# Two-level Strassen gates in the fourth token group of a fused attention and feed-forward kernel

## The chip, the cores and the metric

The kernel runs on one core of one Trainium2 chip. The metric is the device time of one execution in microseconds (us); the time before is the median of three runs. One more execution was taken with the hardware profiler, and all views below are of that one.

## The reference, cut to what matters

Linear attention with a norm, then a feed-forward part whose two gates are multiplied without a nonlinearity. Everything is float32.

```python
# q, k, v: (8, 8, 576, 64); w1, w2: (512, 1024); w3: (1024, 1024); w_out: (1024, 512)
kv  = einsum('bhsd,bhse->bhde', k, v)
out = einsum('bhsd,bhde->bhse', q, kv)
x   = out / sqrt(mean(out * out, -1) + 1e-6) * g_norm
x   = x.transpose(0, 2, 1, 3).reshape(8 * 576, 512)
y   = ((x @ w1) * (x @ w2)) @ w3 @ w_out
```

## The kernel before

**Groups.** Each of the 8 batches gives 512 tokens to a group of its own; the 64 left over of each batch make a ninth group. The groups run in the order T = 0 to 6, then 8 (the left-over tokens), then 7. w3 and w_out are multiplied together once at the beginning (L678). After that each group does two things on TensorE: the *gates* (x times w1 and w2, multiplied with each other on VectorE) and the *projection* (the product times the folded w3 and w_out).

**Gates, one level.** A group has four parts p0 to p3 of the gate columns. `gates` runs each part as one level of a Strassen-Winograd scheme, `winograd`: seven products of 4 matmuls with 256 columns (L699), where seven blocks of the weights (a11, a12, a22 and the sums s1 to s4) meet seven of x (b11, b21, b22, t1 to t4). Between the products ScalarE copies results out of PSUM (`keep`, L712: p1, p5, u2, u3, each into one tile of its name), and VectorE adds and multiplies (L839, L840). The third product, s2 times t2, accumulates in the PSUM bank of the first, so TensorE may only begin it once p1 is kept; in the same way s4 waits for p5, s3 for u2, and a22 for u3. `between` is called twice in each part, after u2 and after c11, and runs the attention work of the next batch, one entry of `steps` at a time.

**Gates, two levels.** For the groups in IN_TWO, now T = 4, 5, 6, 8 and 7, the parts p0 and p1 are done together by `gates_of_two`: each of the seven products is itself split into seven, 49 products of one matmul with 128 columns (L953) for each of the two gates. It is run between parts p2 and p3. It needs sums of sums: those of x are made at the group's beginning (`sum_x`, L918 to L921); those of the weights are made once (`prepare_w`, a triple of vector operations L875, L876, L877 for each of seven products), stored into a scratch tensor w_l2 in DRAM (`store_w`, L868), and loaded back in five pieces for every such group (`load_w`, L899). `replace_a21` (L887) then overwrites the a21 blocks, which only one-level gates still need, with a further sum and stores three of them. Where the triples lie is written out by hand: one each behind the sums of p0, p1 and p2 of T = 2, two each behind p0 and p1 of T = 3; `replace_a21` is called in p2 of T = 3. A triple uses one of three buffers in turn, so that it can only be written when the store of the triple three before has landed. Each of its blocks goes out in a store of its own, 128 KB.

**Projection.** `project_twice` is a two-level scheme for every group but the first: seven times 14 matmuls with 128 columns (L1162). ScalarE copies (L1173, L1174); VectorE makes the sums of its inputs (L1120 to L1124) and finishes the outputs (L1258, L1201, L1202, and four steps L1183 to L1186 for each block of the output). finish(p5), finish(p1) and finish(u4) come last, at the beginning of the next group's gates; the next group's first keep writes the same tile as p1.

**Turns.** q and the attention's x are needed transposed. `turn_by_dma` copies the halves of each float32 apart (L297, L299), has the DMA engines transpose them (L301, on SyncE's queue), and copies them together again (L311). For the batches up to 4 the copies are GpSimd's, except those of batch 1's first half; for later ones they are ScalarE's, hung by `turns_by_scalar` behind named keeps: a key such as (0, 3) is the keep after product 3 of gate 0 in `gates_of_two`, ("p3", "u2") the keep u2 of part 3, ("proj", "u3") a keep of the projection. Batch T + 1 is turned in group T.

**Order.** TensorE, GpSimd and SyncE run in the order of the program. VectorE and ScalarE run in the order that a scheduler gives them, except in part p3 and the projection, where VectorE's order is as written; the scheduler can still put other operations between. `tc.issue_after(x)` holds what is issued in it behind x. Every engine's queue, SyncE's with its DMAs too, is worked off in order.

The lines that place the triples and the first call of `between` in this change:

```python
                with tc.issue_after(ops[-1].ins):
                    for _ in range({(2, 0): 1, (2, 1): 1, (2, 2): 1, (3, 0): 2, (3, 1): 2}.get((T, p), 0)):
                        next(preparing_w)
...
            if T == FIRST_OF_TWO - 1 and p == 2 and not replaced:
                replaced.append(True)
                replace_a21()
```

Of the kernel before, what the change touches and what calls it, by code (L numbers as in the profile page):

```python
# [22 lines left out]
def kernel(  # L23
# [32 lines left out]
    nc = tc.nc  # L56
    PSUM = bass.MemoryType.PSUM
    P = 128
# [3 lines left out]
    DF = w1.shape[1]  # L62
    NP = H // 2
    KF = DF // P
    FIRST_OF_TWO = 4
    NH = KF // 2
    J = 4
    G = J * P
# [19 lines left out]
    loaded, copies, adds = {}, {}, {}  # L88
# [437 lines left out]
    def turns_by_scalar(b):  # L526

        a, turning = batch(b), {}

        def at(key, *call):  # L530
            slots.setdefault(key, []).append(call)

        def begin(name, f, *args):
            turning[name] = f(*args, nc.scalar.copy)
            next(turning[name])
            if name[0] == "q":
                next(turning[name])
            elif name[2]:
                for r in range(2):
                    next(turning["x", name[1], r])  # L540

        def end(name):
            all_of(turning[name])
            if name[0] == "q" and name[1] != "left":
                batch(name[1]).load_ahead("q", name[2])

        for r in (2, 3):
            at((0, 0), begin, ("q", b, r), a.q_by_dma, r)
        if b % 2:
            at(("p2", "c21"), begin, ("q", "left"), a.q_left_by_dma)  # L550
            at((0, 3), end, ("q", "left"))
        at((0, 6), end, ("q", b, 2))
        at((1, 0), end, ("q", b, 3))
        for h, begins, ends in (
            (0, ((0, 3), (0, 3)), ((1, 3), (1, 3))),
            (1, (("p3", "p1"), ("p3", "p5")), (("p3", "c21"), ("proj", "p1"))),
        ):
            for r in range(2):
                at(begins[r], begin, ("x", h, r), a.x_part_by_dma, h, r)
                at(ends[r], end, ("x", h, r))  # L560
        if b + 1 < B:
            n = batch(b + 1)
            for r in range(2):
                at(("p3", "u2"), begin, ("q", b + 1, r), n.q_by_dma, r)
                at(("proj", ("u2", "u3")[r]), end, ("q", b + 1, r))

    def steps(b):

        a = batch(b)
        a.start()
        more = b + 1 < B
        fs, ends = ([[] for _ in range(8)] for _ in range(2))

        def turn(i, f, *args, next_group=False):

            t = []

            def begin():
                t.append(f(*args))
                next(t[0])
                next(t[0])

            fs[i].append((begin,))
            (to_end if next_group else ends[i + 1]).append((lambda: all_of(t[0]),))

        if to_end:

            ends[0] += [(lambda: nc.gpsimd.tensor_copy(tick, late["p5"][:, 0, 0:1]),), *to_end]
        to_end.clear()
        odd = b % 2
        by_scalar = b > FIRST_OF_TWO
        if b == 1:
            early.extend(a.q_two_by_dma(r) for r in (0, 1))
            q_first = list(early)
            fs[0].append((a.begin_kv, 0, 1))

            def end_first():  # L600
                for t in q_first:
                    with tc.issue_after(copies["kv"].ins):
                        next(t)
                    all_of(t)

            ends[1].append((end_first,))
        fs[1] += [(a.begin_kv, 2, 3), (a.finish, 0)]
        if b == 1:
            last = {}

            def begin(name, behind, f, *args):
                last[name] = f(*args)
                with tc.issue_after(copies[behind][-1].ins):
                    next(last[name])
                next(last[name])

            def end(name, behind):
                with tc.issue_after(copies[behind][-1].ins):
                    next(last[name], None)
                all_of(last[name])  # L620

            fs[2] += [(begin, f"q{r}", "u2", a.q_two_by_dma, r) for r in (2, 3)]
            fs[3] += [
                (begin, "x", "u3", a.x_by_dma, 0, nc.scalar.copy),
                (begin, "left", "u3", a.q_left_by_dma),
            ]
            ends[4] += [(end, "q2", "p1"), (end, "q3", "p5"), (end, "x", "u2")]
            ends[5].append((end, "left", "u3"))
        elif by_scalar:
            turns_by_scalar(b)  # L630
        else:
            turn(1, a.q_two_by_dma, 2, 3)
            turn(2, a.x_by_dma, 0)
            if odd:
                turn(1, a.q_left_by_dma)
        second = 5 if b == 1 else 4
        if more:
            fs[second].append((batch(b + 1).begin_kv, 0, 1))
        fs[second].append((a.finish, 1))
        if odd:  # L640
            fs[3 if by_scalar else second].append((a.product_left,))
        if b == 1:
            turn(6, a.x_by_dma, 1)
            turn(7, a.x_left_by_dma, next_group=True)
        else:
            if not by_scalar:
                turn(5, a.x_by_dma, 1)
            if odd:
                turn(5, a.x_left_by_dma, next_group=more)
        if more and not by_scalar:  # L650
            turn(7 if b == 1 else 5, batch(b + 1).q_two_by_dma, 0, 1, next_group=True)
        if more:
            fs[7 if odd else 0].append((load_q_left, b + 1))
        return iter([lambda s=e + f: [f(*args) for f, *args in s] for e, f in zip(ends, fs)])
# [107 lines left out]
    xb, wa, aa, ob = {}, {}, {}, {}  # L762
    xc = const.tile([P, 3, NP // 2, N], FP32, name="xc")
    free = {("w", 0): const.tile([P, 3, 2, NP // 2, P], FP32, name="ws0")}
    o_sbs, ab_sums, w3o_sums, streams, inner_sums = [], [], [], [], []
    PART = 7 * 2 * P

    def allocate():
# [5 lines left out]
    def allocate_projection():  # L774
# [17 lines left out]
            [w[:, 2 * PART:2 * PART + 256], w[:, 2 * PART + 256:2 * PART + 512], room[2][:, PART:PART + 256]],  # L792
        ]
        inner_sums.extend([t.rearrange("p (c t) -> p c t", c=2) for t in s] for s in spare)

    def parts(t):
        return [t[:, i] for i in range(3)]
# [67 lines left out]
    def store_w(n, key, src):  # L865
        dst = w_l2[:, 0:len(BLOCKS) * P].rearrange("p (w m) -> p w m", w=2)
        at = BLOCKS[0, n, key] * P
        nc.sync.dma_start(out=dst[:, :, at:at + P], in_=src)  # L868

    def prepare_w():  # L870

        for n, (name, _) in enumerate(PRODUCTS):
            a11, a12, a21, a22 = w_blocks(name)
            s1, s2, s4 = inner_sums[n % 3]
            nc.vector.tensor_add(s1, a21, a22)  # L875
            nc.vector.tensor_sub(s2, s1, a11)  # L876
            nc.vector.tensor_sub(s4, a12, s2)  # L877
            blocks = {"s1": s1, "s2": s2, "s4": s4, "a11": a11, "a12": a12, "a22": a22}
            for key, t in blocks.items():
                if (0, n, key) in BLOCKS:  # L880
                    store_w(n, key, t)
            yield

    def replace_a21():
        for n, (name, _) in enumerate(PRODUCTS):
            a11, _, a21, _ = w_blocks(name)
            nc.vector.tensor_sub(a21, a11, a21)  # L887
            if (0, n, "s3") in BLOCKS:
                store_w(n, "s3", a21)
# [493 lines left out]
    for n, T in enumerate(groups):  # L1383
        pieces = steps(T + 1) if n + 2 < NG else iter([])

        def between():
            if len(converted) < len(begun):
                with tc.issue_after(copies["u2"][-1].ins):
                    end_next()
            next(pieces, lambda: None)()  # L1390
            if T == 1:
                for _ in range(2):
                    if next(preparing, 0) == 0 and len(loaded_b) < 3:
                        load_b()
            if T == FIRST_OF_TWO - 1 and p == 2 and not replaced:
                replaced.append(True)
                replace_a21()

        if T in IN_TWO:
            p = 2  # L1400
# [9 lines left out]
            of_two = sum_ab_two()  # L1410
            for _ in range(2):
                of_two.pop(0)()
        for p in range(NF):
            if T in IN_TWO and p + 1 < NF:
                continue
            stage[0] = f"p{p}" if T in IN_TWO else None
            if T and p + 1 == NF:
                sum_1, sum_2, sum_4, sum_3 = sum_ab(p)
                following = {
# [50 lines left out]
            else:  # L1470
                ops = [step() for step in sum_ab(p)]
                with tc.issue_after(ops[-1].ins):
                    for _ in range({(2, 0): 1, (2, 1): 1, (2, 2): 1, (3, 0): 2, (3, 1): 2}.get((T, p), 0)):
                        next(preparing_w)
        last = n + 1 == NG
        if T:
            project_twice(
# [4 lines left out]
            continue  # L1482
        project(T, between)
        run(combine_x(1))
        preparing, preparing_w, replaced = prepare_b(), prepare_w(), []
        third = late_pool.tile([P, 3, 2, P], FP32, name="inner_sums")
        inner_sums.append([third[:, i] for i in range(3)])


# [28 lines left out]
```

## Time and profile before

| what | value |
|---|---|
| median of 3 runs | 753.99 us (753.05 to 754.78) |
| the profiled execution | 753.1 us, its span 751.3 us |
| TensorE busy | 743.1 us, 99% of the span |
| VectorE busy | 636.4 us, 85% |
| ScalarE busy | 322.2 us, 43% |
| GpSimd busy | 84.6 us, 11% |
| DMA | 160.94 MB, mean 214 GB/s |
| stores into w_l2 | 33 of 128 KB, 1.8 to 4.2 us to landing |
| DMA transposes L301 | 66, 2.7 to 6.5 us to landing |

How to read it: PE is the matmuls and PEld the weight loads of TensorE, which overlap them; DVE is VectorE, ACT ScalarE, POOL GpSimd, SP SyncE. A line number such as L699 is that of the kernel before. The chain that ended last is followed back from the last instruction to whatever released each one; a share of the span in it is time that can only be won there. An instruction's row has start, duration, engine, line, and in brackets how long its engine had been idle and who released it. Idle time of an engine that isn't on the chain costs nothing.

### The profile page before, as it was taken

Reading aid. Unit: us, or ns where it says so; the run is one execution under the profiler, and the core shown is the slowest. Engines: PE = TensorE matmul, PEld = TensorE weight load, DVE = VectorE, ACT = ScalarE, POOL = GpSimd, SP = SyncE. Lnnn points to the kernel's source line nnn. Section 1 sums busy time; section 2 is a strip of 40 time slices with the busy share of each in tenths; the row PEclk is TensorE's granted clock in tenths of the full one; section 3 lists DMA queues with packets and bytes.
Section 4 is the critical chain, followed back from the end, with each engine's and each line's share of the span. In section 5 each row is a group of like instructions: output and inputs, shape, how many; then the busy total and the mean of one; then the engine's idle time right before and its main releaser. Section 6 shows DMA issues by size and latency. Waiting matters only on the chain.

```text
span 751.3 us, 15612 instructions
## 1 busy us (share of the span) xinstructions
PE 743.1 (99%) x6155; PEld 659.0 (88%) x6155; DVE 636.4 (85%) x1301; ACT 322.2 (43%) x558; POOL 84.6 (11%) x83
## 2 busy tenths in 40 slices
PE   7999999999999999999999999999999999999998
PEld 5455788888899889988999999999999999999997
DVE  6977999648889679877798899889979997899897
ACT  6687878313222332233225753565367323222321
POOL 0000000222520442044201000100001000000000
PEclk9999999999999999999999999999999999999999
DMA  9996955349997947697468986799658663465354
GB/s 306 327 349 193 280 147 118 88 73 280 330 300 264 242 138 207 231 245 217 134 240 228 246 274 225 221 256 259 239 148 208 213 221 108 150 221 177 126 199 140
DMA packets 155245, 160.94 MB, mean 214 GB/s; under 512 B 87076, under 2 KB 140068, under 8 KB 155172
## 3 DMA queue, kind: packets, MB, share of 16 engines
q1 hardware_dynamic: 152720, 145.52, 65.8%
q10 hardware_dynamic: 2452, 14.42, 5.6%
q8 instruction: 49, 0.80, 0.4%
q14 instruction: 24, 0.20, 0.1%
HBM read 121.90 MB, written 20.71 MB: 190 GB/s over the span
## 4 chain that ended last, share of the span: by engine, by line
PE 96%; DMA 2%; DVE 2%; ACT 1%; issue 0%; SPq 0%; ACTq 0%
PE mm L699 45%; PE mm L1162 23%; PE mm L953 15%; PE mm L678 7%; PE at L340 3%; PE at L416 2%; DMA raw<-in_moe_w_out_dram 1%; PE at L665 1%; DMA raw<-in_moe_w_dram 0%; PE at L1213 0%; PE at L435 0%; PE at L359 0%; DVE c L839 0%; DVE chunks L174 0%; DVE inv L385 0%; DVE raw L875 0%
## 5 line engine op out<-in xcount | busy, mean ns | idle before, releaser
L699 PE MATMUL mm<-xT,w_sb 128*128 128x256 f32 x576 | 132.2, 379 | 0.0
L699 PEld LDWEIGHTS mm<-xT,w_sb 128*128 128x128 f32 x576 | 108.7, 190 | 14.8 <-issue 0.5
L699 PE MATMUL mm<-xc,ws 128*128 128x256 f32 x416 | 94.8, 380 | 0.4 <-ACT p L712 0.4
L699 PEld LDWEIGHTS mm<-xc,ws 128*128 128x128 f32 x416 | 78.8, 190 | 12.1 <-ACT p L712 1.5
L678 PE MATMUL mm<-chunks,ab 128*128 128x512 f32 x128 | 60.2, 603 | 1.4 <-DVE chunks L174 1.0
L712 ACT COPY u<-mm 128x512 f32<-128x512 f32 x46 | 27.0, 587 | 74.3 <-PE mm L699 58.9
L712 ACT COPY p<-mm 128x512 f32<-128x512 f32 x54 | 31.5, 586 | 53.2 <-PE mm L699 40.5
L699 PE MATMUL mm<-xc,w_sb 128*128 128x256 f32 x208 | 50.0, 383 | 0.0
L1162 PE MATMUL mm<-w3o_sb,ab 128*128 128x128 f32 x368 | 48.6, 275 | 0.0
L1173 ACT COPY u<-mm 128x512 f32<-128x512 f32 x23 | 13.5, 586 | 81.6 <-DVE raw L1186 47.7
L1162 PE MATMUL mm<-w3o_sb,raw 128*128 128x128 f32 x372 | 48.1, 275 | 0.0
L699 PE MATMUL mm<-xT,ws 128*128 128x256 f32 x192 | 45.8, 381 | 0.0
L1162 PEld LDWEIGHTS mm<-w3o_sb,ab 128*128 128x128 f32 x368 | 45.4, 192 | 0.4
L1162 PEld LDWEIGHTS mm<-w3o_sb,raw 128*128 128x128 f32 x372 | 44.8, 192 | 0.0
L699 PEld LDWEIGHTS mm<-xc,w_sb 128*128 128x128 f32 x208 | 38.9, 190 | 5.5
L678 PEld LDWEIGHTS mm<-chunks,ab 128*128 128x128 f32 x128 | 21.8, 190 | 23.9 <-issue 15.3
L840 DVE TENSOR_TENSOR ab<-c 128x256 f32<-128x256 f32 x78 | 40.7, 522 | 2.1
L385 DVE TENSOR_REDUCE inv<-sq 128x8 f32<-128x512 f32 (+1 forms) x40 | 24.1, 627 | 20.9 <-ACT sq L384 20.6
L834 ACT COPY c<-mm 128x256 f32<-128x256 f32 x26 | 9.7, 372 | 72.6 <-PE mm L699 72.6
L699 PEld LDWEIGHTS mm<-xT,ws 128*128 128x128 f32 x192 | 36.1, 190 | 5.0
L953 PE MATMUL mm<-ws,w3o_sb 128*128 128x128 f32 x250 | 38.5, 275 | 0.0
L297 POOL COPY xT<-xn 128x1024 uint16<-128x1024 uint16 x14 | 17.1, 1249 | 151.5 <-DVE xn L394 151.5
(249 smaller groups left out, 1627.6 us busy)
## 6 DMA issues: line engine op xcount, KB each, us to landing
w3o_sb<-w3o_l SPq DMA_DIRECT2D x18, 896.0 KB, 5.3
raw<-in_moe_w_dram SPq DMA_DIRECT2D x31, 512.0 KB, 7.1
raw<-w3o_l SPq DMA_DIRECT2D x15, 896.0 KB, 4.8
w3o_sb<-w_l SPq DMA_DIRECT2D x15, 896.0 KB, 5.3
w3o_sb<-w3o_l ACTq DMA_DIRECT2D x14, 896.0 KB, 4.6
k_sb<-in_k_dram SPq DMA_DIRECT2D x32, 256.0 KB, 4.5
v_sb<-in_v_dram SPq DMA_DIRECT2D x32, 256.0 KB, 4.8
q_sb<-in_q_dram SPq DMA_DIRECT2D x32, 256.0 KB, 3.6
```

What stands on the lines that cost most here:

```text
L297: copy(to, src.rearrange("p a n w -> p w a n"))
L340: nc.tensor.matmul(kv_ps[e * D:(e + 1) * D, r - rs[0], :], lhsT=k_sb[:, e, cols] if j < J else kl[:, 2 * r + e, :], rhs=v_sb[:, e, cols] i ...
L385: nc.vector.tensor_reduce(out=inv[:, i], in_=sq.rearrange("p (h d) -> p h d", d=D), axis=AX.X, op=ALU.add)
L416: nc.tensor.matmul(o_ps[l][tokens, n * D:(n + 1) * D], lhsT=qT[r][rows, e, i, tokens], rhs=kv_b[rows, e, r, :], start=True, stop=True,)
L678: nc.tensor.matmul(sums_ps[half][m], lhsT=w3T[half, c][:, m, :], rhs=chunks[:, c, 1, :], start=(c == 0), stop=(c == KF - 1),)
L699: nc.tensor.matmul(ps[:, u, :], lhsT=lhsT(a_name, u, c), rhs=rhs(b_name, c),  start=(u == 0 and c == 0 and to is None), stop=(c == chunks ...
L712: copies.setdefault(name, []).append(nc.scalar.copy(t, ps))
L834: copied = nc.scalar.copy(c, one[:, 0, :])
L840: nc.vector.tensor_mul(dst, c[:, 0, :], c[:, 1, :])
L953: nc.tensor.matmul(ps[place // 4][:, place % 4, :], lhsT=x, rhs=y, start=new and place // 4 not in seen, stop=True, skip_group_check=True,)
L1162: nc.tensor.matmul(to[:, i, :], lhsT=x[:, c, :], rhs=y[:, c, :], start=new and place // 4 not in seen, stop=(c == 1), skip_group_check=True,)
L1173: nc.scalar.copy(t[:, 0:4], ps[0])
```

## The change

T = 3 joins the groups with two-level gates (FIRST_OF_TWO is 3). All seven triples are made in T = 2: two at its beginning, two called from the first `between` of p1, three behind the sums of p1; `replace_a21` is called in the second `between` of p2 of T = 2. The sums of a triple now lie in a row in their buffer and go out in one store (in two for the buffer whose third piece lies elsewhere), and a11 with a12 in one: 18 stores instead of 33. For batch 3, turned in the one-level group T = 2, ScalarE gets a list of places of its own for the turns of q and x; batch 4 is turned in T = 3 in the way of the later ones.

```diff
-    FIRST_OF_TWO = 4
+    FIRST_OF_TWO = 3
...
+        if b > FIRST_OF_TWO:
+            q_begins, q_ends = ((0, 0), (0, 0)), ((0, 6), (1, 0))
+            left_q = ("p2", "c21"), (0, 3)
+            x_begins, x_ends = ((0, 3), (0, 3)), ((1, 3), (1, 3))
+        else:
+            q_begins, q_ends = (("p1", "p1"), ("p1", "p5")), (("p1", "u3"), ("p1", "u3"))
+            left_q = ("p0", "c21"), ("p2", "p5")
+            x_begins, x_ends = (("p1", "u2"), ("p1", "u2")), (("p1", "c21"), ("p2", "p1"))
...
-        by_scalar = b > FIRST_OF_TWO
+        by_scalar, in_two = b >= FIRST_OF_TWO, b > FIRST_OF_TWO
...
-        nc.sync.dma_start(out=dst[:, :, at:at + P], in_=src)
+        nc.sync.dma_start(out=dst[:, :, at:at + src.shape[2]], in_=src)
...
-            s1, s2, s4 = inner_sums[n % 3]
+            t = {key: t.rearrange("p (w n) -> p w n", w=2) for key, t in in_a_row[n % 3].items()}
+            s1, s2, s4 = t["s1"][:, :, 0:P], t["s1"][:, :, P:2 * P], t.get("s4", t["s1"])[:, :, -P:]
...
-            blocks = {"s1": s1, "s2": s2, "s4": s4, "a11": a11, "a12": a12, "a22": a22}
-            for key, t in blocks.items():
-                if (0, n, key) in BLOCKS:
-                    store_w(n, key, t)
+            for key in t:
+                store_w(n, key, t[key])
+            if (0, n, "a11") in BLOCKS:
+                store_w(n, "a11", wa[0][name].rearrange("p w c m -> p w (c m)"))
+                store_w(n, "a22", a22)
...
+        def prepare_some(pieces):
+            if T == FIRST_OF_TWO - 1:
+                for _ in range(pieces):
+                    next(preparing_w)
+                prepared.append(pieces)
...
+            if T == FIRST_OF_TWO - 1 and p == 1 and len(prepared) == 1:
+                prepare_some(2)
...
-            if T == FIRST_OF_TWO - 1 and p == 2 and not replaced:
+            if T == FIRST_OF_TWO - 1 and p == 2:
                 replaced.append(True)
-                replace_a21()
+                if len(replaced) == 2:
+                    replace_a21()
...
+        if T == FIRST_OF_TWO - 1:
+            with tc.issue_after(adds["out"].ins):
+                prepare_some(2)
...
-            stage[0] = f"p{p}" if T in IN_TWO else None
+            stage[0] = f"p{p}" if T in IN_TWO or T == FIRST_OF_TWO - 1 else None
...
-                    for _ in range({(2, 0): 1, (2, 1): 1, (2, 2): 1, (3, 0): 2, (3, 1): 2}.get((T, p), 0)):
-                        next(preparing_w)
+                    if p == 1:
+                        prepare_some(3)
```

More of the change, by code (lines that the diff above doesn't have):

```diff
@@ L545, in end @@
                 batch(name[1]).load_ahead("q", name[2])
+        if b > FIRST_OF_TWO:
[6 more added lines that the diff above has]
+            x_begins, x_ends = (("p1", "u2"), ("p1", "u2")), (("p1", "c21"), ("p2", "p1"))
         for r in (2, 3):
-            at((0, 0), begin, ("q", b, r), a.q_by_dma, r)
+            at(q_begins[r - 2], begin, ("q", b, r), a.q_by_dma, r)
         if b % 2:
[L550 to L553, printed above, removed]
+            at(left_q[0], begin, ("q", "left"), a.q_left_by_dma)
+            at(left_q[1], end, ("q", "left"))
+        for r in (2, 3):
+            at(q_ends[r - 2], end, ("q", b, r))
         for h, begins, ends in (
-            (0, ((0, 3), (0, 3)), ((1, 3), (1, 3))),
+            (0, x_begins, x_ends),
             (1, (("p3", "p1"), ("p3", "p5")), (("p3", "c21"), ("proj", "p1"))),
@@ L640, in steps @@
         if odd:
-            fs[3 if by_scalar else second].append((a.product_left,))
+            fs[3 if in_two else second].append((a.product_left,))
         if b == 1:
@@ L764 @@
     free = {("w", 0): const.tile([P, 3, 2, NP // 2, P], FP32, name="ws0")}
-    o_sbs, ab_sums, w3o_sums, streams, inner_sums = [], [], [], [], []
+    o_sbs, ab_sums, w3o_sums, streams, inner_sums, in_a_row = [], [], [], [], [], []
     PART = 7 * 2 * P
@@ L794, in allocate_projection @@
         inner_sums.extend([t.rearrange("p (c t) -> p c t", c=2) for t in s] for s in spare)
+        in_a_row.append({"s1": room[1][:, 1024:PART]})
+        in_a_row.append({"s1": w[:, 2 * PART:2 * PART + 512], "s4": spare[1][2]})
     def parts(t):
@@ L1484 @@
         run(combine_x(1))
-        preparing, preparing_w, replaced = prepare_b(), prepare_w(), []
+        preparing, preparing_w, prepared, replaced = prepare_b(), prepare_w(), [], []
         third = late_pool.tile([P, 3, 2, P], FP32, name="inner_sums")
         inner_sums.append([third[:, i] for i in range(3)])
+        in_a_row.append({"s1": third.rearrange("p s c t -> p (s c t)")})
 _INS = ['q', 'k', 'v', 'g_norm', 'moe_w1', 'moe_w2', 'moe_w3', 'moe_w_out']
```

## The prediction

> **What bounds the kernel now.** I read the page's rows of busy time and its chain first, then the chain in order of time to find where each group begins and ends, then the busy time of each engine by group, and last the instructions in order of time around the places that the change touches. Groups are named by T; the fourth is T = 3, the third T = 2.
>
> ```profile
> PE 743.1 (99%) x6155; PEld 659.0 (88%) x6155; DVE 636.4 (85%) x1301; ACT 322.2 (43%) x558; POOL 84.6 (11%) x83
> PE 96%; DMA 2%; DVE 2%; ACT 1%; issue 0%; SPq 0%; ACTq 0%
> ```
>
> TensorE is the bound: 96% of the chain that ended last is its own work. So a gain has to be TensorE work removed, and a cost is a place where TensorE has to wait. The next view gives busy time by group, T = 1 to T = 6 (T = 3 is the third row, T = 5 the fifth):
>
> ```profile
> 163.00:239.30 76.30, 76.30 (x633) 69.61 (x632) 62.09 (x126) 20.39 (x43) 20.46 (x19) 1.00 0.99 292
> 239.27:315.78 76.51, 76.38 (x662) 69.33 (x661) 60.35 (x126) 21.24 (x46) 22.48 (x20) 1.00 0.72 200
> 315.78:391.85 76.07, 75.71 (x629) 68.74 (x629) 60.67 (x127) 20.18 (x43) 22.42 (x19) 1.00 0.73 209
> 391.85:465.90 74.05, 74.05 (x745) 70.30 (x745) 67.73 (x149) 41.26 (x70) 4.42 (x4) 1.00 0.82 234
> 465.90:539.05 73.15, 73.15 (x713) 69.58 (x713) 65.09 (x146) 38.87 (x65) 2.43 (x3) 1.00 0.81 240
> 539.05:611.71 72.66, 72.66 (x705) 68.97 (x705) 66.32 (x151) 36.45 (x62) 2.32 (x3) 1.00 0.70 211
> ```
>
> After stretch and length come PE, PEld, DVE, ACT and POOL busy. The granted clock is 1.00 in all. TensorE fills every group; the fourth has only 0.36 us of idle. T = 5 is what the fourth group is turned into: also a group before an even batch, with the same attention work on TensorE (no left-over rows), two-level gates, turns on ScalarE. It is 2.92 us shorter. The chain in order of time shows where:
>
> ```profile
> 239.27 10.60 PE mm L699 x48
> ...
> 350.77 19.19 PE mm L699 x88
> 369.96 21.88 PE mm L1162 x196
> 391.85 10.36 PE mm L699 x48
> ...
> 480.59 15.63 PE mm L953 x140
> ```
>
> Counts are matmuls and weight loads together, so 88 is 44 matmuls of 256 columns at 436 ns, and 140 is 70 matmuls of 128 columns at 223 ns.
>
> **The change, part by part.**
>
> *Gates of the fourth group.* Gone are 2 parts x 7 products x 4 = 56 matmuls of 256 columns (L699): 56 x 0.436 = 24.4 us. New are 2 x 49 = 98 of 128 columns (L953): 98 x 0.223 = 21.9 us. That is -2.5 us. The Trainium skill speaks against this step: "TensorE: Matmul & The Clock Gate", section "Back-to-back issue gap", gives a stream of load-and-multiply pairs about 81 ns at 128 columns and 131 ns at 512, so half the columns cost far more than half the time. Interpolated, 256 columns would be 98 ns, a ratio of 0.83, and the estimate from that page is 98 x 0.436 x 0.83 = 35.5 us: 11 us slower. In this trace's stream the ratio is 223/436 = 0.51, in five groups of the same code. I take the trace. The direct difference of whole groups, T = 5 against T = 3, is 73.15 - 76.07 = -2.92 us; it holds the -2.5, the 0.36 us of waiting that the fourth group has now (below), and rounding. I take -2.92.
>
> Beside TensorE in that group: five loads of stored gate sums (5.3 us to landing, three of them issued a projection ahead), the sums of x (L918 to L921, eight vector operations, about 5 us) and ScalarE's turns (41 against 20 us busy). All of it runs in T = 4 to 6 with TensorE at 100%, so I cost it at nothing.
>
> *The sums of the weights.* Seven triples (L875 to L877) and seven L887 are made, as now; but four triples and all L887 leave the fourth group for the third. One operation takes 0.42 us and the next starts 0.34 us later, so the third group's VectorE gains 19 x 0.34 = 6.5 us: 60.35 becomes about 67 of 76.5, and 67.73 of 74.05 works in T = 4. What leaves is what made the fourth group wait 0.36 us: there the triples, L887 and GpSimd's copies meet, and L875 takes 1.26 us instead of 0.42 while a copy runs.
>
> Where the operations lie decides. The order of the changed program puts one triple (inner_sums, L875 to L877) into the end of the second group's projection, between L1258 and L1186 of finish(p5); then come finish(p1), finish(u4), two more triples and the third group. This stretch is already late:
>
> ```profile
> 240.43 0.29 DVE L1183 TENSOR_TENSOR p<-p 128x128 f32<-128x128 f32 x1
> ...
> 241.55 0.42 DVE L1186 TENSOR_TENSOR raw<-p 128x256 f32<-128x256 f32 x1
> ...
> 242.06 1.29 ACT L712 COPY p<-mm 128x512 f32<-128x512 f32 x2 [2.27 <-DVE raw L1186]
> ...
> 242.70 1.59 PEld L699 LDWEIGHTS mm<-xc,ws 128*128 128x128 f32 x8 [0.37 <-ACT p L712]
> ```
>
> The third group's first keep (p1) may only overwrite its tile when finish(p1) has read it (L1186), and the product s2 waits for that keep. There is no slack: it is why T = 2 opens with 10.60 us where T = 4 has 10.36. So each us put ahead of this L1186 is a us of TensorE. Three operations at 0.34 are 1.02 us at most. At least it is 0.68: between dependent steps VectorE now loses 0.12 (L1258 to L1183), 0.11 (L1183 to L1184) and 0.11 us (L1184 to L1185), which the new ones fill. I take +0.68, because the two sequences interleave one by one. The two other triples follow finish(u4) and end near 246.9; L839, which needs them out of the way, is due at 247.2 with TensorE itself 0.7 later. Without that margin they would cost up to 2 us.
>
> The triple in part 0 replaces one that is there now. The last three triples, L836, L753 and three L887 (14 operations, 4.8 us) fall into 268.4 to 273.2; VectorE waits there today until 274.56 (4.45 us idle), so they are hidden.
>
> *Stores.* 33 of 128 KB (2.0 us to landing) become 18 of up to 384 KB. No row is of that shape; bounds are 2.0 us and the 4.9 us of the 384 KB store to w3o_l. I take about 4, nearer the latter. SyncE issues fewer: 15 x 0.4 us less. A store matters where a triple reuses a buffer: the one in part 0 at about 250.5 needs the store issued at 246 (landing 250); the last two need stores issued at 264 to 266 (landing by 270), used at 269 to 271. Cost 0, up to 0.5 us.
>
> *Turns of q and x.* Most of GpSimd's 20 and 19 instructions in T = 2 and T = 3 go to ScalarE: in T = 2 it has 21 us and gets 14 copies of 1.05 to 1.17 us. TensorE allows a keep (0.59 us) one product of 1.74 us, so one copy fits after each keep, and two after u2 and u3, where the next keep is 3.5 us away. SyncE's transposes take 1.26 us to issue, 3.0 to land. From today's times: the left-over q begins at 254.9, q at 256.6 and 258.2, x at 259.9; q lands at 260.7 and 262.3, x at 264 and 265. The copies back come at 263.5 (q) and 266.7 (x). So about 1.2 us to spare for q and 2 for x. Behind a late one stand c21 and p1 of the next part, with another 1.9 us. I take 0. The slowest transposes of the trace took 6.5 us, 3.5 more than reckoned, which would cost between 0 and 1.5 us; a gain isn't possible, since TensorE isn't waiting there.
>
> **Sum.** -2.92 + 0.68 = -2.24 us. The profiled execution took 753.1 us (span 751.3), so 750.9. The median of the runs, 753.99, is 0.9 us higher; from it, 751.8.
>
> **Rivals.**
> - *The inserted triple costs nothing* (it slips into waits, and p1 is as late as now): -2.92, 751.1. For it: finish(p5) is a dependent chain. Against: only 0.34 us of bubbles. Chance 0.06.
> - *The third group takes most back*: transposes or stores land later than reckoned, or one keep is pushed over its 1.14 us of slack. 1 to 2 us: 752.8 to 753.8, 753.2 in the middle. For it: ScalarE's order in part 1 is packed so closely that after u3 only 0.5 us is free before c21. Against: T = 4 to 6 run the same turns without a wait. Chance 0.23.
> - *Slower: SyncE's one queue ties the three engines together.* In part 1 a transpose waits for ScalarE's copy, the stores of the third and fourth triple stand behind the transposes, VectorE's triples six and seven wait for these stores to land, and behind them in VectorE's order are the reductions of the next norm and L839, for which keeps wait. It decides when the store lands after about 274 (269 by my times, 1.3 us of slack before L385 at 274.56 and 2 more before u3's keep); from there each us is one us, and 278 undoes the gain and ends above 755.5. I put it at 756. Against: it needs 8 to 9 us of delay. Chance 0.11.
> - My forecast: 0.60.
>
> **Numbers.** 0.2% (1.5 us) is about what can be told from no change. Faster: 0.66 (forecast and first rival); same 0.23; slower 0.11. The forecast's own range is 751.0 to 752.5. The range to 754.2 takes in the second rival, 750.7 the first, and leaves out the slower case and little else.
>
> **What would show it.** T = 3 at 73.0 to 73.4 us with 98 matmuls on L953 shows the gates right. The third group's first stretch at 11.2 to 11.6 instead of 10.60, its first keep waiting for L1186 near 242.7, shows the inserted triple. No wait of TensorE for a keep in parts 1 and 2 shows the turns hidden; a wait there, with ScalarE idle for a transpose or VectorE idle for a store, is the second or third rival. L875 at 0.42 us throughout shows that GpSimd is out of the way. If T = 3 is not shorter by 2.5 us or more, the forecast is wrong at its root.

## The result, and the profile after

| | before | after |
|---|---|---|
| median of 10 runs | 753.4 us (752.63 to 754.78) | 750.81 us (750.02 to 752.35) |
| ratio | | 0.9966, 95% interval 0.9957 to 0.9976 |
| span of the profiled execution | 751.3 us | 750.6 us |
| first weight load of T = 2 to the end of the span | 512.3 us | 510.0 us |
| T = 2, from its first weight load to the first matmul of T = 3 | 76.78 us | 77.35 us |
| T = 3, between first matmuls | 76.07 us | 73.16 us |

The first matmul of a group is dated as in the chain in order of time, here and below.

The medians differ by 2.6 us (the interval: 1.8 to 3.2). The two spans differ by 0.7 us only, because T = 2 began 1.64 us later in the profiled execution of after. TensorE waited 2.4 us for the first converted weights there, where it waited 1.0 us before, and behind that wait the granted clock was 0.50 for 3.4 us (before, then after; behind stretch and length come PE, PEld, DVE, ACT and POOL busy with their instructions, then the granted clock, the DMA's busy share and GB/s):

```profile
11.92:15.33 3.41, 3.09 (x14) 1.86 (x13) 3.10 (x6) 2.00 (x3) 0.00 (x0) 1.00 1.06 378
11.92:15.33 3.41, 3.41 (x5) 1.24 (x4) 3.31 (x7) 1.23 (x3) 0.00 (x0) 0.50 1.07 376
```

Both differ between executions of one kernel: in e9 below, which is the changed kernel again, the wait was 1.0 us and the clock 1.00. The three of the ten runs of the changed kernel whose mean granted clock was 0.997 are its three longest, 751.70 to 752.35 us; the other seven took 750.02 to 750.91. So I compare T = 2 and T = 3 alone, which together are 2.34 us shorter. Line numbers from here on are those of the changed kernel: L699 is now L707, L712 L720, L839 L849, L840 L850, L868 L878, L875 to L877 are L886 to L888, L953 L965, L1162 L1174, L1183 to L1186 are L1195 to L1198. In the views of e2 the lines behind the triple stand four higher, in those of e5 and e8 the lines from L879 on one higher.

The page of after, TensorE and chain:

```profile
PE 741.5 (99%) x6239; PEld 659.6 (88%) x6239; DVE 640.5 (85%) x1339; ACT 358.8 (48%) x598; POOL 42.7 (6%) x48
PE 97%; DVE 1%; DMA 1%; ACT 1%; SPq 0%; issue 0%; ACTq 0%
```

GpSimd's busy time has halved, ScalarE has its copies, VectorE has hardly changed, and TensorE is the bound as before. The busy time by group, T = 2 and T = 3 (after stretch and length: PE, PEld, DVE, ACT, POOL):

```profile
240.64:317.99 77.35, 76.67 (x664) 69.56 (x663) 62.28 (x144) 39.11 (x64) 4.14 (x4) 1.00 0.78 229
317.99:391.15 73.16, 73.16 (x714) 69.59 (x713) 64.41 (x144) 38.92 (x65) 2.25 (x3) 1.00 0.78 236
```

T = 3 is filled to the last by TensorE and is as long as T = 5 was. T = 2 has 0.68 us in which TensorE had nothing to do. The instructions in order of time at the beginning of T = 2 show where it is:

```profile
239.30 0.42 DVE L886 TENSOR_TENSOR inner_sums<-ws 128x256 f32<-128x256 f32 x1
239.84 0.41 DVE L887 TENSOR_TENSOR inner_sums<-inner_sums,ws 128x256 f32<-128x256 f32 x1
240.51 0.41 DVE L888 TENSOR_TENSOR inner_sums<-ws,inner_sums 128x256 f32<-128x256 f32 x1
...
243.82 0.41 DVE L1198 TENSOR_TENSOR raw<-p 128x256 f32<-128x256 f32 x1
...
244.33 1.08 ACT L720 COPY p<-mm 128x512 f32<-128x512 f32 x2 [2.90 <-DVE raw L1198]
...
244.97 1.59 PEld L707 LDWEIGHTS mm<-xc,ws 128*128 128x128 f32 x8 [1.00 <-ACT p L720]
244.97 1.99 PE L707 MATMUL mm<-xc,ws 128*128 128x256 f32 x8 [0.60 <-ACT p L720]
```

The triple lies ahead of L1198, the keep waits for L1198, the product s2 waits for the keep. The weight load's wait was 0.37 us before and is 1.00 us now.

### The profile page after: what moved, and what is told of

Read it like the earlier page. It is cut to its first block, busy times and chain, and to the rows that moved or that the text cites. A ratio compares the mean times of both kernels' runs of the same rounds, so it can differ in the third digit from the quotient of the medians.

```text
span 750.6 us, 15799 instructions
## 1 busy us (share of the span) xinstructions
PE 741.5 (99%) x6239; PEld 659.6 (88%) x6239; DVE 640.5 (85%) x1339; ACT 358.8 (48%) x598; POOL 42.7 (6%) x48
## 4 chain that ended last, share of the span: by engine, by line
PE 97%; DVE 1%; DMA 1%; ACT 1%; SPq 0%; issue 0%; ACTq 0%
PE mm L707 42%; PE mm L1174 23%; PE mm L965 18%; PE mm L686 7%; PE at L340 3%; PE at L416 2%; PE at L673 1%; DMA raw<-in_moe_w_out_dram 1%; PE at L1225 0%; PE at L435 0%; ACT kv_sb L351 0%; PE at L359 0%; DVE chunks L174 0%; SPq L199 0%; ACT chunks L162 0%
## 5 line engine op out<-in xcount | busy, mean ns | idle before, releaser
L707 PE MATMUL mm<-xT,w_sb 128*128 128x256 f32 x528 | 121.2, 379 | 0.0
L707 PEld LDWEIGHTS mm<-xT,w_sb 128*128 128x128 f32 x528 | 99.5, 190 | 13.5 <-issue 0.5
L707 PE MATMUL mm<-xc,ws 128*128 128x256 f32 x384 | 87.3, 380 | 0.6 <-ACT p L720 0.6
L707 PEld LDWEIGHTS mm<-xc,ws 128*128 128x128 f32 x384 | 72.8, 190 | 11.2 <-ACT p L720 1.4
L720 ACT COPY u<-mm 128x512 f32<-128x512 f32 x42 | 24.6, 586 | 61.2 <-PE mm L707 47.8
L720 ACT COPY p<-mm 128x512 f32<-128x512 f32 x50 | 29.2, 586 | 45.9 <-PE mm L707 33.5
L1174 PE MATMUL mm<-w3o_sb,ab 128*128 128x128 f32 x368 | 48.6, 275 | 0.0
L1174 PE MATMUL mm<-w3o_sb,raw 128*128 128x128 f32 x372 | 48.1, 275 | 0.0
L965 PE MATMUL mm<-ws,w3o_sb 128*128 128x128 f32 x300 | 46.2, 275 | 0.0
L707 PE MATMUL mm<-xc,w_sb 128*128 128x256 f32 x192 | 46.2, 383 | 0.0
L1174 PEld LDWEIGHTS mm<-w3o_sb,ab 128*128 128x128 f32 x368 | 45.4, 192 | 0.4
L1174 PEld LDWEIGHTS mm<-w3o_sb,raw 128*128 128x128 f32 x372 | 44.8, 192 | 0.0
L707 PE MATMUL mm<-xT,ws 128*128 128x256 f32 x176 | 41.9, 381 | 0.0
L385 DVE TENSOR_REDUCE inv<-sq 128x8 f32<-128x512 f32 (+1 forms) x40 | 24.3, 628 | 19.6 <-ACT sq L384 19.5
L707 PEld LDWEIGHTS mm<-xc,w_sb 128*128 128x128 f32 x192 | 35.8, 190 | 5.1
L965 PEld LDWEIGHTS mm<-ws,w3o_sb 128*128 128x128 f32 x300 | 39.8, 192 | 0.0
L707 PEld LDWEIGHTS mm<-xT,ws 128*128 128x128 f32 x176 | 33.2, 190 | 4.6
L850 DVE TENSOR_TENSOR ab<-c 128x256 f32<-128x256 f32 x72 | 34.9, 485 | 1.9
```

Source lines behind the costliest of these rows:

```text
L385: nc.vector.tensor_reduce(out=inv[:, i], in_=sq.rearrange("p (h d) -> p h d", d=D), axis=AX.X, op=ALU.add)
L707: nc.tensor.matmul(ps[:, u, :], lhsT=lhsT(a_name, u, c), rhs=rhs(b_name, c),  start=(u == 0 and c == 0 and to is None), stop=(c == chunks ...
L720: copies.setdefault(name, []).append(nc.scalar.copy(t, ps))
L850: nc.vector.tensor_mul(dst, c[:, 0, :], c[:, 1, :])
L965: nc.tensor.matmul(ps[place // 4][:, place % 4, :], lhsT=x, rhs=y, start=new and place // 4 not in seen, stop=True, skip_group_check=True,)
L1174: nc.tensor.matmul(to[:, i, :], lhsT=x[:, c, :], rhs=y[:, c, :], start=new and place // 4 not in seen, stop=(c == 1), skip_group_check=True,)
```

## The experiments

The theory: the gain is that of the matmuls, less the triple that lies ahead of the first keep of T = 2. Its rivals: the gain comes from taking GpSimd's copies and the sums out of the fourth group; or the loss in T = 2 comes from the turns or the stores. All the numbers of T = 2 below are from its first weight load to the first matmul of T = 3. They are of one profiled execution each; the medians are of all runs, each set beside the kernel before on its own chip.

| run | first keep: PEld waits | wait in part 1 | T = 2 | T = 3 | median; ratio to the kernel before, 95% interval |
|---|---|---|---|---|---|
| before | 0.37 | none | 76.78 | 76.07 | |
| after | 1.00 | none | 77.35 | 73.16 | 750.81; 0.9966 (0.9957 to 0.9976) |
| e1_held | 0.24 | 1.57 | 78.03 | 73.15 | 751.24; 0.9973 (0.9961 to 0.9985) |
| e2_twice | 1.31 | none | 77.66 | 73.16 | 751.04; 0.9968 (0.9955 to 0.998) |
| e3_one_level | 1.00 | none | 77.36 | 75.44 | 752.66; 0.999 (0.9982 to 0.9999) |
| e4_pool_turns | 0.68 | 1.36 and 2.62 | 80.80 | 73.14 | 753.3; 1.0004 (0.9992 to 1.0017) |
| e5_small_stores | 0.67 | none | 77.03 | 73.15 | 750.37; 0.9961 (0.9948 to 0.9975) |
| e6_third_in_p1 | 0.35 | 1.60 | 78.16 | 73.16 | 750.72; 0.9962 (0.9949 to 0.9974) |
| e7_both_in_p1 | none | none | 76.49 | 73.16 | 750.4; 0.9959 (0.9947 to 0.9972) |
| e8_third_small | none | 2.06 | 78.42 | 73.15 | 751.59; 0.9976 (0.9967 to 0.9986) |
| e9_changed_again | 1.00 | none | 77.36 | 73.15 | 750.39; 0.9961 (0.9948 to 0.9975) |
| e10_both_again | none | none | 76.49 | 73.15 | 750.67; 0.9965 (0.9953 to 0.9978) |

**The gates put back.** The edit keeps all the rest of the change:

```diff
-    IN_TWO = (*range(FIRST_OF_TWO, B - 1), *TWICE)
+    IN_TWO = (*range(FIRST_OF_TWO + 1, B - 1), *TWICE)
-        if b > FIRST_OF_TWO:
+        if b > FIRST_OF_TWO + 1:
-            stage[0] = f"p{p}" if T in IN_TWO or T == FIRST_OF_TWO - 1 else None
+            stage[0] = f"p{p}" if T in IN_TWO or T in (FIRST_OF_TWO - 1, FIRST_OF_TWO) else None
```

Here T = 3 reads a21 blocks that replace_a21 has overwritten in T = 2, so its parts compute something else than the reference's, with the same instructions.

> The change without its core: the fourth group's gates stay at one level, with the triples all in T = 2, the merged stores and the turns of batches 3 and 4 on ScalarE (batch 4 in the places of batch 3). Theory: the gain is the matmuls alone. T = 3 then takes 75.6 to 75.8 us (76.07 before, less its 0.36 us of waiting), T = 2 77.1 as in the changed kernel, and the time is about that of the kernel before: 0 to +0.5 us over it (ratio 1.000 to 1.001). Rival: the gain comes from taking GpSimd's copies and the sums out of the fourth group. Then T = 3 falls to 75 us or less and the time stays under that of the kernel before by 1 us or more.

The chain in order of time, T = 3 from 316.29 to 391.73:

```profile
316.29 10.36 PE mm L707 x48
...
369.85 21.89 PE mm L1174 x196
391.73 10.36 PE mm L707 x48
```

T = 3 took 75.44 us: 2.28 us more than with two levels. So the matmuls are 2.28 of the 2.91 us, and 0.63 us come from what left the group. That is more than the 0.3 to 0.5 us that I had expected, yet much less than the rival wanted; how it divides between the triples and GpSimd's copies no run shows. By the trace this kernel is level with the kernel before (512.3 us from the first weight load of T = 2 to the end, as before). Its median is 0.46 us under it, with an interval that reaches from 0.1 to 1.4 us, where I had expected 0 to 0.5 us over it. The matmuls carry the gain.

**The triple counted twice, and held back.** In the first kernel the triple at the end of the projection is computed a second time; in the second it and the next are held behind c12 of part 0.

```diff
             nc.vector.tensor_sub(s4, a12, s2)
+            if n == 2:
+                nc.vector.tensor_add(s1, a21, a22)
+                nc.vector.tensor_sub(s2, s1, a11)
+                nc.vector.tensor_sub(s4, a12, s2)
```

```diff
             if T == FIRST_OF_TWO - 1 and p == 1 and len(prepared) == 1:
-                prepare_some(2)
+                with tc.issue_after(adds["c12"][-1].ins):
+                    prepare_some(2)
```

> The changed kernel with the third triple computed twice with the same values; the second copy also lies ahead of the last step of finish(p1). Theory: each operation put there is passed on to TensorE, at 0.2 to 0.34 us each. The wait for the first keep of T = 2 grows from 0.60 to 1.3 us (1.2 to 1.6), T = 2 from 77.1 to 77.8 us, the time by 0.7 us over the changed kernel's. Rival: there is slack at that place. Then nothing moves.

> The changed kernel with its third and fourth triple held behind the first c12 of T = 2, so that no triple lies in the second group's projection any more. Theory: the triple ahead of finish(p1) is the only thing that the change costs. Then TensorE's wait for the first keep of T = 2 falls from 0.60 us to about 0 (its weight load from 1.00 to about 0.4, as before the change), T = 2 takes 76.5 us instead of 77.1, and the time is 0.6 us shorter than the changed kernel's, 2.9 to 3.1 under the kernel before (ratio about 0.996). Rival: the 0.6 us in T = 2 come from ScalarE's turns or the stores. Then T = 2 stays at 77.1 us and TensorE waits elsewhere.

With the triple twice, the instructions in order of time:

```profile
242.98 1.07 ACT L720 COPY p<-mm 128x512 f32<-128x512 f32 x2 [3.21 <-DVE raw L1202]
...
243.61 1.59 PEld L707 LDWEIGHTS mm<-xc,ws 128*128 128x128 f32 x8 [1.31 <-ACT p L720]
```

1.31 us looks like 0.31 more than after. But VectorE doesn't come out of the second group's work at the same distance each time: the addition p5 + u3 (L1258, L1270 or near it) begins 2.33 to 2.46 us ahead of the first weight load of T = 2 in the profiled executions of before, after, e1, e3, e6 and e9, 2.65 to 2.67 us in those of e2, e4, e5, e7 and e8, and 3.60 us in e10. At 2.66 us one triple makes the load wait 0.67 (e5) and 0.68 (e4), two make it wait 1.31; at 2.34 us none makes it wait 0.37 (0.35 in e6), and one 1.00 (after, e3, e9). So the first triple costs 0.63 and the second 0.64 us: three operations pass on 0.21 us each. The rival, slack at that place, is out.

Held back, the first keep is as early as before the change (0.24 us), and yet T = 2 was 0.68 us longer than in the changed kernel. My expectation failed: the fourth triple, one place further forward in part 0 now, waited there 2.44 us for a store, and the first keep of part 1 came late (1.57 us). What made that wait so long is taken up with e6.

**Where a triple may stand.** Two more versions hold the triples behind the c21 of part 0, where they come to lie behind the norm: in e6 the third alone, in e7 the third and the fourth. In e6 the fourth moves forward by one place, ahead of L850, by the scheduler's choice.

```diff
             if T == FIRST_OF_TWO - 1 and p == 1 and len(prepared) == 1:
-                prepare_some(2)
+                with tc.issue_after(adds["c21"][-1].ins):
+                    next(preparing_w)
+                prepare_some(1)
```

(in e7: `prepare_some(2)` inside the `with`, and nothing after it)

> The changed kernel with its third triple alone held behind the c21 of part 0, where it lies behind the norm's last step and no longer in the second group's projection; the fourth triple stays in part 0. Theory: the wait for the first keep of T = 2 falls from 1.00 to about 0.3 us (PEld) without a new one, because in part 1 VectorE waits for TensorE anyway; T = 2 takes 76.8 us instead of 77.36, and the time is 0.6 us under the changed kernel's. Rival, from the first held version: any triple in parts 0 and 1 is in the way of a keep. Then a wait of 0.5 us or more comes up in part 1, and T = 2 stays at 77.3 us or more.

> As the last, with the fourth triple behind the norm too, so that part 0 has no triple and no wait for a store. Theory: the same 76.8 us, since the fourth triple's wait for the first store (0.96 us in the changed kernel) was covered. If instead that wait held the first keep of part 1 back, T = 2 gets shorter than in the last run, by up to 0.3 us. Rival: six operations between the norm and c12 of part 1 are too many, and keep u3 of part 1 waits; T = 2 above 77.2 us.

e6, in order of time:

```profile
246.07 0.37 SPq L878 DMA_DIRECT2D w_l<-raw  x1
...
251.52 0.42 DVE L886 TENSOR_TENSOR raw<-ws 128x256 f32<-128x256 f32 x1 [3.00 <-DMA w_l<-raw]
251.86 0.42 DVE L850 TENSOR_TENSOR ab<-c 128x256 f32<-128x256 f32 x1
...
256.11 0.31 ACT L389 ACTIVATE inv<-inv,eps_col 128x16 f32<-128x16 f32 x1 [2.46 <-DVE inv L385]
256.32 1.03 ACT L299 COPY qT_left<-ql_sb 128x1024 uint16<-128x1024 uint16 x1
...
257.26 0.58 ACT L720 COPY p<-mm 128x512 f32<-128x512 f32 x1
...
257.89 1.59 PEld L707 LDWEIGHTS mm<-xc,ws 128*128 128x128 f32 x8 [1.60 <-ACT p L720]
```

This is a chain through four queues: the store of the first triple, issued at 246.07, frees the buffer at 251.5; VectorE stands still until then, with c22, c11 and the norm's reductions behind L886; ScalarE's L389 waits for the reductions; the turn of the left-over q and the keep stand behind L389; the weight load waits for the keep. My expectation of no new wait failed; the rival's wait of 0.5 us or more came. In the changed kernel the same L886 comes one place later, and waits as well, but less:

```profile
249.31 0.37 SPq L878 DMA_DIRECT2D w_l<-raw  x1
...
253.18 0.43 DVE L886 TENSOR_TENSOR raw<-ws 128x256 f32<-128x256 f32 x1 [0.96 <-DMA w_l<-raw]
```

There the keep of part 1 ended at 259.16; the weight load that needs it began at 259.55, the matmul at 259.76. Some 0.4 us were left.

The place alone doesn't make the difference. In e5, further below, the triple lies at the same place as in e6, waits 1.14 us, and TensorE loses nothing in part 1. What differs is when the store lands: 11.9 us after the first weight load of T = 2 in e5, 12.5 in the changed kernel, 13.3 in e1 and 13.4 in e6, although e6 issued it 0.65 us earlier than the changed kernel. The reductions (L385) begin 15.49 us after that weight load in the changed kernel and 16.75 in e6. Of the 1.26 us between them 0.92 are the later landing, and 0.34 the one operation more that lies behind the triple. And since TensorE waits 0.65 us less for its first keep in e6, it comes to part 1 that much earlier. Why the store landed later in e1 and e6 is open.

With both triples behind the norm (e7) no wait is left in T = 2, and the rival's late keep of u3 didn't come:

```profile
241.85 3.21 PEld L707 LDWEIGHTS mm<-xc,ws 128*128 128x128 f32 x15
242.97 0.59 ACT L720 COPY p<-mm 128x512 f32<-128x512 f32 x1 [1.96 <-DVE raw L1198]
```

The weight loads of s1 and s2 run through as one row, and T = 2 takes 76.49 us, 0.86 us less than in the changed kernel. Some 0.3 of this is VectorE's earlier start in that execution. In the time less is seen: the medians of e6 and e7, from one chip, differ by 0.3 us, where their traces of T = 2 differ by 1.67. So the wait in the profiled execution of e6 need not be its usual size.

**Stores.** Cut into 128 columns again, alone (e5) and with the third triple behind the norm (e8):

```diff
-        nc.sync.dma_start(out=dst[:, :, at:at + src.shape[2]], in_=src)
+        for i in range(0, src.shape[2], P):
+            nc.sync.dma_start(out=dst[:, :, at + i:at + i + P], in_=src[:, :, i:i + P])
```

> The changed kernel with its stores cut into pieces of 128 columns again, 33 of 128 KB instead of 18, in the same places. Theory: the number of stores is not on TensorE's path, since SyncE has room and the transposes of q and x stand ahead of the stores of the third and fourth triple. T = 2 stays within 0.1 us of 77.36 us (from the first weight load of T = 2 to that of T = 3), T = 3 at 73.15, the time within 0.3 us of the changed kernel's. Rival: fewer stores keep SyncE's queue ahead of the turns. Then a transpose or a triple comes later, and T = 2 grows by 0.5 us or more.

> The version with the third triple alone behind the norm, with its stores cut into pieces of 128 columns. In that version the fourth triple waited 3.00 us for the 384 KB store of the first, and the first keep of part 1 held TensorE for 1.60 us (PEld). Theory: the wait is the landing of the large store, which the fourth triple's first operation doesn't need whole. With 128 KB pieces it needs the first piece only, so that its wait falls to 2 us or less, the wait of TensorE in part 1 to 0.5 us or less, and T = 2 from 78.16 to 77.0 us or less. Rival: the store is late because it is issued late or stands behind other transfers, whatever its size. Then the fourth triple still waits 2.5 us or more, and T = 2 stays at 77.8 us or more.

e5: T = 2 took 77.03 us, outside the 0.1 us that I had allowed; the 0.3 us to 77.35 are VectorE's earlier start, by which the first keep waits 0.67 us instead of 1.00. Nearly twice as many stores cost nothing that can be seen. In e8 the fourth triple waited longer still, 3.58 us, and part 1 lost 2.06:

```profile
251.38 0.42 DVE L887 TENSOR_TENSOR raw<-ws 128x256 f32<-128x256 f32 x1 [3.58 <-DMA w_l<-raw]
...
258.80 1.59 PEld L707 LDWEIGHTS mm<-xc,ws 128*128 128x128 f32 x8 [2.06 <-ACT p L720]
```

The scheduler put that triple one place further forward than in e6, ahead of L849. Here the place does cost: the store landed nearly as in the changed kernel (12.6 against 12.5 us after the first weight load of T = 2), but from the triple's beginning to the reductions it takes 4.34 us, where the changed kernel has 2.95 and e6 3.29.

The size of the store isn't the cause, and my expectation fell. In all eleven runs of the changed order the first store out of `raw` lands 11.3 to 13.4 us after that weight load, although it is issued between 4.5 and 9.0 us after it: 128 KB took 8.1 us in e8 and 6.8 in e5, 384 KB 3.8 in the changed kernel. What is issued ahead of it on the same queue lands first: the 896 KB load of w3o_sb 8.6 to 10.6 us after that weight load, the output's second store after 10.7 to 12.7, and the triple's store in every run 0.3 to 1.3 us behind the output's. That fits the rival, a store that stands behind other transfers; that it would land earlier without them no run shows. Later in T = 2 the size can be seen: the store of the third triple, issued some 26 us after that weight load, took 2.74 us in one piece of 384 KB, and the pieces of 128 KB in e5 took 1.97 and 1.98 us, the last landing at the same 29.0 us.

**The turns left to GpSimd.**

```diff
-        by_scalar, in_two = b >= FIRST_OF_TWO, b > FIRST_OF_TWO
+        by_scalar, in_two = b > FIRST_OF_TWO, b > FIRST_OF_TWO
```

> The changed kernel with the turns of batch 3 in T = 2 left to GpSimd, as before. Theory: moving them to ScalarE is there to keep VectorE's sums at 0.42 us; with GpSimd copying, operations with two inputs in SBUF take 1.1 to 1.4 us, and the fourteen operations at the end of part 1 and the sums in part 0 overrun the room that they have. T = 2 grows by 0.3 to 2 us over 77.1 us. Rival: ScalarE's turns cost TensorE time in T = 2. Then T = 2 gets shorter than 77.1 us without them.

```profile
256.82 1.23 POOL L299 COPY qT_left<-ql_sb 128x1024 uint16<-128x1024 uint16 x1
257.07 1.25 DVE L888 TENSOR_TENSOR raw<-ws,raw 128x256 f32<-128x256 f32 x1
...
260.37 1.59 PEld L707 LDWEIGHTS mm<-xc,ws 128*128 128x128 f32 x8 [1.36 <-ACT p L720]
...
285.27 0.73 PEld L707 LDWEIGHTS mm<-xc,w_sb 128*128 128x128 f32 x4 [2.62 <-ACT u L720]
```

T = 2 took 80.80 us in the profiled execution, 3.45 more than with the turns on ScalarE. The median, 753.3 us, was back at that of the kernel before on that chip, 753.12, so the whole gain was gone. The eight runs whose granted clock was 1.00 went from 751.79 to 754.80, so the loss varies. The direction was as expected, the size of T = 2 nearly twice the upper end. The first wait, 1.36 us in part 1, is the expected one: L888 takes three times as long while GpSimd copies, and the sums of part 0 and the reductions behind them end late. The larger one, 2.62 us for the keep of u3, came mainly by another way. The chain in order of time has it:

```profile
267.00 2.63 POOL xT L297 x2
...
269.65 1.24 SPq L301
...
274.15 4.61 DMA w_l<-raw
...
278.78 0.44 DVE raw L886
...
280.33 1.20 DVE inv L385 x2
...
284.64 0.59 ACT u L720
```

GpSimd copies x until 269.63. The transposes wait for that copy, and the stores of the third and fourth triple stand behind the transposes in SyncE's queue: they are issued at 272.30 and 274.15, where the changed kernel has 266.88 and 268.72. The sixth and the seventh triple wait 1.78 and 0.62 us for them to land, the seventh until 278.78; the reductions stand behind it, and the keep of u3 behind the reductions. This is the slower rival of the prediction, step by step, with GpSimd in ScalarE's place. It had named a landing at 278 us as the one that undoes the gain; this one came at 278.75, with T = 2 beginning 1.4 us later than before the change.

**The version without a wait beside the changed kernel.**

> The changed kernel itself, as a yardstick for the two others on the same chip. About 0.34% under the kernel before; T = 2 at 77.35 us, or 77.05 where VectorE comes out of the second group 0.3 us earlier, as it does in some executions.

> The version with the third and fourth triple both behind the norm, beside the changed kernel on the same chip. Theory: T = 2 is 0.6 us shorter than in the changed kernel (at the same start of VectorE), 76.5 to 76.8 us, and the time is 0.3 to 0.6 us lower. Rival: no difference in the time that can be told.

In the traces T = 2 is 77.36 against 76.49 us. In the time no difference can be told: 750.39 against 750.67 us, intervals 0.9948 to 0.9975 and 0.9953 to 0.9978. My expectation of 0.3 to 0.6 us in the time failed. The first weight load of T = 2, ahead of which the two kernels do the same work on TensorE, came at 238.08 in one and at 240.15 us in the other (1.03 us of this is a wait of TensorE for VectorE in the projection before, at 233.93, which e7, the same kernel as e10, doesn't list); a difference of 0.9 us is lost in that.

## Why the prediction was right

It forecast -2.24 us, and 751.8; the medians moved by 2.6 us, T = 2 and T = 3 of the traces by 2.34. The median of 750.81 lies just under the forecast's own range, 751.0 to 752.5, and inside the wider one that takes in the first rival; about 0.6 of the 1.0 us to 751.8 are that the median before is 753.4 over ten runs, not 753.99. The interval of the medians, 1.8 to 3.2 us, can't tell the forecast from the first rival (-2.92: the inserted triple costs nothing). The traces can, and they decide for the forecast.

- *The gates, -2.92.* T = 3 went from 76.07 to 73.16 us, -2.91. Choosing the trace's rows over the interpolated estimate of 11 us on the other side was right: 98 short matmuls were no slower than their columns. The split of the sum was off. The matmuls are 2.28 us, not 2.5: I had multiplied by the 436 ns of a stretch that has attention work at both of its ends; 28 matmuls in 12.09 us, 432 ns, give 24.2 - 21.9 = 2.3. What left the group was worth 0.63, not 0.36 us: TensorE's row showed 0.36 us of idle, its weight loads 0.76, and the loss lies between. It did so in T = 2 as well: without any wait (e7, e10) T = 2 takes 76.49 us, and the wait listed as 0.60 and 1.00 us made it 77.35, 0.86 longer. One reading was wrong without a consequence: the counts in the chain are matmul records alone, two for each matmul of the program, and not matmuls and weight loads together.
- *The triple ahead of the first keep, +0.68.* Measured 0.63 us (0.37 to 1.00), and 0.64 for a second one. It went in full to TensorE, at the place and through the chain that were named. T = 2 grew by 0.57 us. VectorE's work in T = 2 I had let grow by 6.5 us; it grew by 1.9 (60.35 to 62.28).
- *The two triples at the beginning of T = 2.* I let them end at 246.9 and L839 begin on time. GpSimd's last copy of q, which stays there, made two of their operations last 1.37 us instead of 0.42:

```profile
245.68 2.65 POOL L311 COPY qT<-q_sb 128x1024 uint16<-128x1024 uint16 x2
...
245.95 1.37 DVE L886 TENSOR_TENSOR w3o_sb<-w_sb 128x256 f32<-128x256 f32 x1
...
247.25 1.37 DVE L887 TENSOR_TENSOR raw<-raw,w_sb 128x256 f32<-128x256 f32 x1
...
249.54 0.68 DVE L849 TENSOR_TENSOR c<-mm,u 128x512 f32<-128x512 f32 x1
```

  L849 began 8.90 us after the first weight load of T = 2, where 7.53 (before) and 0.63 us of TensorE's own delay make 8.16. These 0.7 us cost nothing, because u3's keep wasn't due yet.
- *The stores, 0.* I took 4 us to landing; the store that the fourth triple needed took 3.8. VectorE still waited 0.96 us for it, because it was issued 8.7 us after the first weight load of T = 2 and not 7 (246, as reckoned). TensorE lost nothing, with some 0.4 us to spare: that the cost came out at 0 was luck in part. e1 and e6 show what such a wait costs where the store lands a little later, e8 where the triple lies two places earlier. My slower rival had this mechanism (a store, a triple behind it, the norm, a keep), but at the end of part 1, where the stores cost 0.34 us of VectorE's time and nothing of TensorE's. With the copies left on GpSimd it came about there (e4).
- *The turns, 0.* No keep in parts 1 and 2 made TensorE wait.

The small surplus of the medians over the traces (0.3 us) is inside the interval.

## What to carry to other kernels

When a group of a kernel is to be turned into the form of another, the neighbour that already has that form gives the gain better than instruction counts do; what remains to be worked out is the way of the moved work, operation by operation in the order of each queue. A stage that starts with an engine running late has no slack: what a scheduler slips in ahead of the late engine's last step is passed on in full, 0.63 us here for three operations that look free at 85% busy. And before an operation is moved forward, look at the buffer it writes: held up by a store, it holds up all that stands behind it, and the end of that chain can be another engine's copy a part further on.

## What the runs showed of the hardware

Operations of VectorE with two inputs in SBUF took 1.25 to 1.41 us instead of 0.42 while GpSimd copied (L886 to L888 in the changed kernel and in e4).

When a store landed depended on what was issued ahead of it. Stores of 128 KB took 1.9 to 8.1 us in e8, those of 384 KB 2.7 to 5.1 us in T = 2 of the changed kernel.

A wait of TensorE costs more than the idle time in the row of its matmuls and less than that in the row of its weight loads: 0.60 and 1.00 us for a loss of 0.86 (after), 0.91 and 1.31 for 1.17 (e2), against the 76.49 us of T = 2 in e7 and e10.

TensorE's wait for the converted weights at the very beginning ranged from 0.2 (e6) to 2.4 us (after) among the profiled executions. In three of the twelve (after, e4, e7) the granted clock was 0.50 for 3.4 us, from about 12 us on; in the other nine it was 1.00 there. Both shift everything after them, and together they hide a change of 0.6 us in the time of one execution.
